# Sliding attention beside a gated MLP on one core: block 2 summed before the tensor engine, an earlier start of the value stage, a fixed port order, and outputs by accumulating DMA

## The chip, the cores and the metric

The kernel runs on one core of a Trainium2 chip. The metric is device time in microseconds (us); most executions agree within 0.3%. The trace names the engines PE (TensorE, matrix products; PEld is its weight load), DVE (VectorE), ACT (ScalarE), POOL (GpSimd) and SP (SyncE, which issues DMAs). "L930" is line 930 of that kernel's program; the same work has another line number in another version, so the text names the work with the line.

## The reference

One layer norm feeds two branches, and both are added to x. The tensors are 2048 positions by 640 features, in bf16.

```python
def reference(A_x, A_wqkv, A_wo, B_x, B_w_gate, B_w_up, B_w_down):
    x = A_x
    xn = _layernorm(x)
    return x + attention(xn, A_wqkv, A_wo) + mlp(xn, B_w_gate, B_w_up, B_w_down)

# attention (shortened): 32 heads of 20 features; position s looks at
# s, s-2, s-4, ... s-14 (8 places), softmax over these 8, then @ wo
# mlp: (xn @ w_gate) * (xn @ w_up) @ w_down, with 1536 hidden features
```

## The kernel before

The program is built by a small list scheduler in Python: it keeps an expected clock for each engine and emits tasks in an order fixed at build time. On the chip each engine runs its own list in that order and waits on semaphores. The 2048 positions are four blocks j of 512; the 640 features are five chunks c of 128.

Logits: VectorE multiplies queries by shifted keys (8 places as two rows r of 4), and TensorE sums the 20 features of a head with a 0/1 matrix `G` of 32 columns. Four such matmuls lie side by side in the array, one for each 128 positions. In the "narrow" way each chunk gives a product tile that goes to TensorE, ten tiles for a block. In the "wide" way, used for block 3 only, VectorE makes fp32 products straight from the queries in PSUM (the memory into which TensorE writes), GpSimd and accumulating DMAs add chunks 0 to 3, and TensorE gets four tiles: two sums and two of chunk 4.

```python
QUAD = {3: (1, 0)}                       # blocks whose rows 1 and 0 go the wide way
ORDER = ((0, "n"), (1, "n"), (2, "n"), (3, "n"), (3, "w"))
...
# logits(j, slots): four tiled matmuls for each product tile
for a in range(4):
    o = PS[32 * a:32 * a + 32, b, :].rearrange("p (q s) -> p q s", q=4)
    ... e.matmul(o, G[:], x, ..., tile_position=(0, 32 * a))
```

Values: after a softmax (one for blocks 0 and 1, one for 2 and 3) VectorE multiplies attention by values for each of 20 units (one unit is a block and a chunk), GpSimd adds the two rows of places, and TensorE sums the remaining four with a 0/1 matrix `SEL`, in batches of units.

```python
BATCH = (1, 4, 9, 14, 19)                # last unit of each batch of value sums
def calm():                              # GpSimd keeps off while a softmax has begun
    return all(("sm", x) in done or count.get(("logits", x), 0) < 2 for x in range(2))
```

Output: for each tile of 128 positions, `dn` runs 12 matmuls with `w_down` and 5 with `wo` into one PSUM bank; VectorE adds x (`fin`, out of a small ring `XR`) into `FOUT`, and a DMA stores it.

## Time and profile before

| | before |
|---|---|
| device time, median of 4 | 268.65 us (268.47 to 268.70) |
| span of the profiled execution | 266.8 us |
| first projection matmul starts | 6.21 us |
| last add of an output starts | 264.27 us |
| busy: PE, VectorE, ScalarE, GpSimd | 98%, 82%, 40%, 50% |
| tiled runs on PE (4 of logits, 5 of value sums) | 9 |

A "tiled run" here is an unbroken stretch of matmuls with `G` or `SEL`, between full-width matmuls. The busy share says which engine has the least room, but not whether PE's matmuls are fast; for that one divides a stretch's time by its matmuls. The chain that ended last tells which work sets the end. The lines are in the prediction below.

### The profile page before, as it was taken

The numbers are of one execution on the slowest core, as the hardware profiler recorded it, in microseconds if no ns is written. First come the engines' busy times: TensorE is split into PE (matmuls) and PEld (weight loads), VectorE is DVE, ScalarE is ACT, GpSimd is POOL, SyncE is SP. The second block draws the span as 40 slices with busy tenths as digits, with TensorE's granted clock in tenths as the row PEclk, the third lists the DMA queues.
The fourth block names the chain that finished last, engine by engine and source line by source line (L and its number), as shares of the span: only waits on it lengthen the run. The fifth ranks groups of instructions, "written<-read, shape, count | busy, mean of one in ns | idle before, by whom it ended". The sixth has DMA issues, their size and how long they took to land.

```text
span 266.8 us, 4468 instructions
## 1 busy us (share of the span) xinstructions
PE 261.3 (98%) x1771; PEld 152.6 (57%) x1788; DVE 218.3 (82%) x278; ACT 107.6 (40%) x193; POOL 132.4 (50%) x83
## 2 busy tenths in 40 slices
PE   7999999999999999999999999999999999999996
PEld 5996965444444444444444446764577547754775
DVE  4678899999999996379999899988998999981221
ACT  3469998556732122255434442007500460016000
POOL 1000000000007359700399999977999799979000
PEclk9999999999999999999999999999999999999999
DMA  7974789502226997193426733656345633130101
GB/s 213 374 207 81 195 107 371 213 0 98 101 49 161 192 234 178 9 333 81 114 49 142 170 80 87 185 162 168 80 129 152 184 96 89 49 98 2 49 27 49
DMA packets 40933, 35.75 MB, mean 134 GB/s; under 512 B 16080, under 2 KB 39120, under 8 KB 40912
## 3 DMA queue, kind: packets, MB, share of 16 engines
q1 hardware_dynamic: 40096, 33.31, 46.0%
q0 software_dynamic: 576, 2.10, 4.1%
q8 instruction: 14, 0.23, 0.4%
q10 hardware_dynamic: 240, 0.05, 0.1%
q14 instruction: 7, 0.06, 0.1%
HBM read 25.07 MB, written 5.26 MB: 114 GB/s over the span
## 4 chain that ended last, share of the span: by engine, by line
PE 96%; DVE 1%; DMA 1%; issue 1%; ACT 0%
PE PS L1195 39%; PE PS L1277 28%; PE PS L655 22%; PE PS L930 3%; PE PS L687 2%; PE PS L1144 2%; DMA XST<-in_A_x_dram 1%; PE PS L599 0%; DVE STATS L542 0%; ACT XNT L611 0%; DVE XNS L563 0%; DVE XNT L609 0%; DVE FOUT L1290 0%; ACT SD L548 0%; DVE MV L545 0%
## 5 line engine op out<-in xcount | busy, mean ns | idle before, releaser
L1096 POOL TENSOR_TENSOR SV<-PV 128x1024 bf16<-128x1024 f32 x40 | 93.2, 2361 | 20.4 <-DVE LOG L981 19.4
L1091 DVE TENSOR_TENSOR PV<-VX,PS 128x1024 f32<-128x1024 bf16 (+1 forms) x56 | 91.9, 1669 | 2.5 <-POOL SV L1096 2.3
L655 PE MATMUL PS<-XNT,WQKV 128*128 128x512 bf16 (+2 forms) x384 | 60.2, 315 | 0.4 <-issue 0.2
L1195 PE MATMUL PS<-XNT,WG 128*128 128x512 bf16 x238 | 59.4, 379 | 0.2
L1195 PE MATMUL PS<-XNT,WU 128*128 128x512 bf16 x231 | 57.7, 379 | 0.4 <-issue 0.2
L655 PEld LDWEIGHTS PS<-XNT,WQKV 128*128 128x128 bf16 x390 | 37.9, 112 | 21.8 <-ACT LOG L941 0.8
L1195 PEld LDWEIGHTS PS<-XNT,WG 128*128 128x128 bf16 x240 | 23.3, 98 | 28.5 <-issue 0.8
L1195 PEld LDWEIGHTS PS<-XNT,WU 128*128 128x128 bf16 x240 | 23.4, 98 | 28.2 <-ACT LOG L941 0.4
L819 DVE TENSOR_TENSOR PRD<-QT,KT 128x2048 bf16<-128x2048 bf16 x32 | 36.8, 1215 | 0.0
L1290 DVE TENSOR_TENSOR FOUT<-PS,XR 128x320 bf16<-128x320 f32 (+1 forms) x33 | 15.7, 477 | 18.4 <-PE PS L1277 18.3
L1277 PE MATMUL PS<-WD,HT 128*128 128x320 bf16 x192 | 28.5, 299 | 0.0
L660 ACT ACTIVATE HT<-PS 128x512 bf16<-128x512 f32 x24 | 14.3, 596 | 31.6 <-PE PS L1195 31.6
L1277 PE MATMUL PS<-WO,OT 128*128 128x320 bf16 (+1 forms) x165 | 26.6, 295 | 0.0
L890 POOL TENSOR_TENSOR PRF<-PRF,PRF 128x1024 f32<-128x1024 f32 x4 | 9.4, 2348 | 31.2 <-DVE PRF L864 31.2
L660 ACT ACTIVATE UX<-PS 128x512 bf16<-128x512 f32 x14 | 8.4, 597 | 39.5 <-PE PS L1195 39.5
L949 POOL MEMSET LOG<- 32x6 bf16 (+6 forms) x7 | 0.4, 96 | 47.6 <-ACT LOG L941 47.6
L1204 DVE TENSOR_TENSOR HT<-HT,PS 128x512 bf16<-128x512 bf16 x23 | 15.7, 684 | 9.5 <-PE PS L1195 7.4
L1277 PEld LDWEIGHTS PS<-WD,HT 128*128 128x128 bf16 x192 | 18.6, 98 | 8.0 <-issue 0.4
L1277 PEld LDWEIGHTS PS<-WO,OT 128*128 128x128 bf16 x165 | 15.9, 98 | 5.9
L864 DVE TENSOR_TENSOR PRF<-PS,KT 128x1024 f32<-128x1024 f32 x16 | 19.0, 1216 | 0.3 <-DMA PRF<-PRF 0.3
L660 ACT ACTIVATE XNT<-PS 128x512 bf16<-128x512 f32 x12 | 7.2, 598 | 25.5 <-PE PS L1195 25.5
L542 DVE BATCH_NORM_STATS2 STATS<-XST 128x6 f32<-128x320 bf16 x32 | 14.6, 472 | 2.5 <-DMA XST<-in_A_x_dram 2.5
(62 smaller groups left out, 235.7 us busy)
## 6 DMA issues: line engine op xcount, KB each, us to landing
VX<-v_scratch SPq DMA_DIRECT2D x80, 130.0 KB, 2.9
XST<-in_A_x_dram SPq DMA_DIRECT2D x16, 160.0 KB, 5.7
v_scratch<-VST SPq DMA_DIRECT2D x4, 640.0 KB, 4.2
XR<-in_A_x_dram SPq DMA_DIRECT2D x16, 160.0 KB, 2.7
out_dram<-FOUT SPq DMA_DIRECT2D x15, 160.0 KB, 1.8
PRF<-PRF POOLq DMA_DIRECT2D x4, 512.0 KB, 8.7
WG<-in_B_w_gate_dram SPq DMA_DIRECT2D x1, 1920.0 KB, 8.6
WU<-in_B_w_up_dram SPq DMA_DIRECT2D x1, 1920.0 KB, 12.0
```

The costliest lines, as they stand in the source:

```text
L542: op("dve", lambda e: e.bn_stats(o, a), r=[a], w=[("st", t, i)], name=f"bn{t}_{i}", occ=0.49)
L655: op("pe", (lambda o, l, x, c, first: lambda e: e.matmul(o, l, x, start=first, stop=(c == NCH - 1)))(o, l, x, c, first), r=[l, x], w=[o], ...
L660: X = op("act", (lambda o, i: lambda e: e.activation(o, i, ACT.Copy))(o, i), r=[i], w=[o], name=name, occ=0.12 + n * 0.9e-3)
L819: op("dve", lambda e: e.tensor_tensor(s[:], qb, kv, ALU.mult), r=[q, rk], w=[s[:]], name=f"prod{j}_{r}_{c}", occ=1.15, lock=True)
L864: X = op("dve", lambda e: e.tensor_tensor(o[:], qb, kv, ALU.mult), r=[q, rk], w=[o[:]], name=f"prow{j}_{r}_{c}_{q0}", occ=1.17)
L890: yield Task("pool", lambda: op("pool", lambda e: e.tensor_tensor(x, x, y, ALU.add), r=[x, y] + tokens(), w=[x], name=name, occ=2.36, lock ...
L1091: op("dve", lambda e: e.tensor_tensor(p, vw, a, ALU.mult), r=[vv] + rk, w=[p], name=f"pv{u}_{x}_{r0}", occ=0.09 + 1.1 * nr)
L1096: X = op("pool", lambda e: e.tensor_tensor(o, p[:, :, 0, :], p[:, :, 1, :], ALU.add), r=[p[:]] + tokens(), w=[o], name=f"pva{u}_{x}", occ= ...
L1195: op("pe", (lambda l, x, c: lambda e: e.matmul(PS[:, b, :], l, x, start=(c == 0), stop=(c == NCH - 1)))(l, x, c), r=[l, x], w=[PS[:, b, :] ...
L1204: X = op("dve", lambda e: e.tensor_tensor(h, h, PS[:, hold[1], :], ALU.mult), r=[h, PS[:, hold[1], :]], w=[h], name=f"h{m}_{j}", occ=0.65)
L1277: op("pe", (lambda l, x, i: lambda e: e.matmul(dst, l, x, start=(i == 0), stop=(i == n - 1)))(l, x, i), r=[l, x], w=[PS[:, b, :]], name=f" ...
L1290: X = op("dve", lambda e: e.tensor_tensor(o, PS[:, b, 0:wid], xr, ALU.add), r=[PS[:, b, :], xr], w=[o], name=f"fin{t}_{nb}", occ=0.15 + wi ...
```

## The change

The intent is fewer matmuls for block 2's logits. The diff is long; this is its core, and cuts are marked. "Port" in it means the memory port that VectorE and GpSimd share (point (3) of what the prediction cites).

```diff
-    QUAD = {3: (1, 0)}
+    QUAD = {2: (1, 0), 3: (1, 0)}
-    ORDER = ((0, "n"), (1, "n"), (2, "n"), (3, "n"), (3, "w"))
+    ORDER = ((0, "n"), (1, "n"), (2, "n"), (3, "n"), (2, "w"), (3, "w"))
...  # fixed port order: a "lock" operation waits for the other engine's last one
+        if lock:
+            deps.update({d.idx: d for d in self.port["pool" if eng == "dve" else "dve"]})
...  # values ahead of softmax 2: GpSimd may work if it ends before VectorE needs the port
-    def calm():
-        return all(("sm", x) in done or count.get(("logits", x), 0) < 2 for x in range(2))
+    def room(occ, ready=0.0):
+        def f():
+            if count.get(("logits", 0), 0) >= 2 and ("sm", 0) not in done:
+                return False
+            return due[0] == INF or max(K.t["pool"], K.t_lock, ready) + occ <= due[0] + SLIP
+        return f
+    calm = room(2.36)
-    BATCH = (1, 4, 9, 14, 19)
+    BATCH = (1, 4, 6, 9, 11, 14, 19)
...  # outputs of blocks 0 to 2: x copied to the output once, results added by DMA
+        def copy_x():
+            ... op("sp", lambda e: e.dma_start(o, i), w=[("outx",)], dma=True, name="outx", nbytes=2e6)
+        def fin_act():
+            K.free_bank(hold[0], evac([(o, PS[:, hold[0], 0:wid], wid)], f"fin{t}_{nb}"))
+        def add_out():
+            ... e.dma_start(d, f, accum_op=ALU.add), r=[f, ("outx",)]
+            if j < 3:
+                yield Task("act", fin_act, r=[PS[:, hold[0], :]], w=[o], prio=6)
+                return
...  # square roots of the layer norm in pairs of tiles, SEL built on GpSimd, new buffers
```

More of the change, by code (lines that the diff above doesn't have):

```diff
@@ L64, in __init__ @@
         self.t_lock = 0.0
+        self.port = {"dve": [], "pool": []}
         self.t_data = 0.0
@@ L122, in deps_of @@
             for q in rds:
-                if inorder and q.eng == eng and not q.dma and eng != "dve":
+                if inorder and q.eng == eng and not q.dma and eng != "dve" and not (eng == "act" and k[0] == "ps"):
                     continue
@@ L195, in op @@
                 X.event = (g[0], 16)
+        if lock:
+            self.port[eng] = [X] if eng == "dve" else self.port[eng] + [X]
+            if eng == "dve":
+                self.port["pool"] = []
         self.ops.append(X)
@@ L391, in build_kernel @@
     SV += [sb("SV3", [128, 4, JB], at=a_qk + 33024), sb("SV4", [128, 4, JB], at=a_qk + 33024 + 4096)]
-    SV += [sb(f"SV{5 + i}", [128, 4, JB], at=a_ra + i * 4096) for i in range(3)]
-    sv_free = list(range(NS))
+    SV += [sb("SV5", [128, 4, JB], at=a_ra + 6 * D * 2)]
+    sv_free = [3, 4, 0, 1, 2]
     a_sc = place[0]
@@ L414, in build_kernel @@
     PRD32 = [K.sbuf(f"PRF{i}", [128, 2, JB], FP32, K.base[p.name]) for i, p in enumerate(PRD)]
-    QUAD = {3: (1, 0)}
+    QUAD = {2: (1, 0), 3: (1, 0)}
     BY_DMA = (((0, 0), (0, 2)), ((1, 0), (1, 2)))
-    NXR = 3
     a_xr = place[0]
-    XR = sb("XR", [128, NXR, D])
-    FOUT = sb("FOUT", [128, 2, D])
+    FB0 = sb("FB0", [128, 5, D])
+    FB1 = sb("FB1", [128, 2, D], at=a_ra)
+    XR = sb("XR", [128, 4, D], at=a_ra + 2 * D * 2)
     NXN = 5
@@ L440, in ht @@
             return XNT[:, m % NCH, m // NCH * JB:(m // NCH + 1) * JB]
-        return HX[HXM[m]][:] if j == 2 else HT[:, j, m, :]
+        if j == 2:
+            return OT[:, 3, m - 8, :] if m >= 8 else HX[HXM[m]][:]
+        return HT[:, j, m, :]
     HXM = (0, 1, 2, 3, 8, 9, 10, 11, 4, 5, 6, 7)
@@ L474, in build_kernel @@
        r=[IDENT[:]], w=[IDENT[:]], name="ident", occ=0.4)
+    op("pool", lambda e: e.memset(SEL[:], 0.0), w=[SEL[:]], name="sel", occ=0.1)
+    for q in range(4):
+        op("pool", (lambda q: lambda e: e.affine_select(SEL[:], SEL[:], pattern=[[-1, 32]], compare_op=ALU.not_equal, fill=1.0,
+                                                        base=-32 * q, channel_multiplier=1))(q),
+           r=[SEL[:]], w=[SEL[:]], name=f"sel{q}", occ=0.2)
     op("pool", lambda e: e.memset(G[:], 0.0), w=[G[:]], name="g0", occ=0.2)
@@ L518, in loads @@
         yield t(w, WU, B_w_up)
+        def copy_x():
+            a, b = ohbm[0:3 * JB, :], xhbm[0:3 * JB, :]
+            o, i = a.rearrange("(p r) n -> p (r n)", p=128), b.rearrange("(p r) n -> p (r n)", p=128)
+            op("sp", lambda e: e.dma_start(o, i), w=[("outx",)], dma=True, name="outx", nbytes=2e6)
+        yield num(2, "lg")
+        yield t(copy_x)
     def late_loads():
@@ L545, in aggr @@
             op("dve", lambda e: e.bn_aggr(mv, st), r=[("st", t, 0), ("st", t, 1)], w=[("mv", t)], name=f"bnag{t}", occ=0.2)
+        ts = next((g for g in GROUPS if t in g), (t,))
+        t0, t1 = ts[0], ts[-1] + 1
         def sqrt():
-            op("act", lambda e: e.activation(sd, mv[:, 1:2], ACT.Sqrt, bias=EPSC[:, 0:1]), r=[("mv", t), EPSC[:]],
-               w=[("sd", t)], name=f"sd{t}", occ=0.25)
-            mark("sd", t)
+            o, i = SD[:, t0:t1, 0:1], MV[:, t0:t1, 1:2]
+            op("act", lambda e: e.activation(o, i, ACT.Sqrt, bias=EPSC[:, 0:1]), r=[("mv", k) for k in ts] + [EPSC[:]],
+               w=[("sd", k) for k in ts], name=f"sd{t}", occ=0.25)
+            for k in ts:
+                mark("sd", k)
         def recip():
-            op("dve", lambda e: e.reciprocal(rstd, sd), r=[("sd", t)], w=[("rstd", t)], name=f"rstd{t}", occ=0.16)
-            mark("rstd", t)
+            o, i = SD[:, t0:t1, 1:2], SD[:, t0:t1, 0:1]
+            op("dve", lambda e: e.reciprocal(o, i), r=[("sd", k) for k in ts], w=[("rstd", k) for k in ts], name=f"rstd{t}", occ=0.16)
             if t >= N_DVE_A:
-                op("dve", lambda e: e.tensor_scalar(nmr, mv[:, 0:1], rstd, -1.0, op0=ALU.mult, op1=ALU.mult),
-                   r=[("mv", t), ("rstd", t)], w=[("nmr", t)], name=f"nmr{t}", occ=0.13)
+                n, m = SD[:, t0:t1, 2:3], MV[:, t0:t1, 0:1]
+                op("dve", lambda e: e.scalar_tensor_tensor(n, m, -1.0, o, op0=ALU.mult, op1=ALU.mult),
+                   r=[x for k in ts for x in (("mv", k), ("rstd", k))], w=[("nmr", k) for k in ts], name=f"nmr{t}", occ=0.13)
+            for k in ts:
+                mark("rstd", k)
         def apply():
@@ L584, in front @@
         yield Task("dve", aggr, r=[("st", t, 1)], prio=p)
-        yield Task("act", sqrt, r=[("mv", t)], prio=p - 1)
-        yield Task("dve", recip, r=[("sd", t)], prio=p)
+        mark("mv", t)
+        if t == ts[-1]:
+            yield Task("act", sqrt, r=[("mv", t)], prio=p - 1)
+            yield Task("dve", recip, r=[("sd", t)], prio=p)
+        yield have("rstd", t)
         if t >= NXN:
@@ L777, in slot @@
         return n
-    def calm():
-        return all(("sm", x) in done or count.get(("logits", x), 0) < 2 for x in range(2))
+    INF = 1e9
+    due = [INF]
+    def room(occ, ready=0.0):
[5 more added lines that the diff above has]
+    calm = room(2.36)
     def tokens():
-        return [("tok", x) for x in range(2) if ("sm", x) in done]
+        return []
     def k_view(j, r, c, q0, nq):
@@ L793, in products @@
         holds = {}
-        for j, kind in ORDER:
+        for at, (j, kind) in enumerate(ORDER):
             if kind == "w":
@@ L799, in products @@
             else:
-                if len(QUAD.get(j, ())) == 2 and j not in holds:
+                if len(QUAD.get(j, ())) == 2 and j not in holds and (j, "w") == ORDER[at + 1]:
                     yield from fetch(j, 0, holds.setdefault(j, {c: [] for c in range(4)}))
@@ L806, in products @@
                 K.spawn(logits(j, rows[j]))
+        mark("products")
     def narrow(j, r, c, slots):
@@ L833, in copy @@
         def copy():
-            evac([(QT[:, j, c, :], PS[:, hold[0], :], JB)], f"qev{j}_{c}")
+            o, i = QT[:, j, c, :], PS[:, hold[0], :]
+            op("act", lambda e: e.activation(o, i, ACT.Copy), r=[i], w=[o, ("qev", j, c)], name=f"qev{j}_{c}", occ=0.58)
             for _ in range(4):
@@ L855, in wide @@
                     yield lambda: len(hold[c]) > 0 and len(usable(j)) > 0
+                    yield num(4, "qk", 0, j, c)
                     k = slot(j)
@@ L863, in go @@
                     def go(o=o, qb=qb, kv=kv, q=q, rk=rk):
-                        X = op("dve", lambda e: e.tensor_tensor(o[:], qb, kv, ALU.mult), r=[q, rk], w=[o[:]],
+                        X = op("dve", lambda e: e.tensor_tensor(o[:], qb, kv, ALU.mult), r=[q, rk, ("qev", j, c)], w=[o[:]],
                                name=f"prow{j}_{r}_{c}_{q0}", occ=1.17)
@@ L929, in go @@
                     x = s[:, :, a * TS:(a + 1) * TS]
-                    op("pe", (lambda o, x, i, a: lambda e: e.matmul(o, G[:], x, start=(i == 0), stop=(i == nt - 1),
-                                                                   tile_position=(0, 32 * a)))(o, x, i, a),
+                    op("pe", (lambda o, x, i, a, nt: lambda e: e.matmul(o, G[:], x, start=(i == 0), stop=(i == nt - 1),
+                                                                   tile_position=(0, 32 * a)))(o, x, i, a, nt),
                        r=[G[:], x], w=[o], name=f"lg{j}_{r}_{i}_{a}", occ=0.054, lat=0.4, mode=1)
@@ L958, in tt, with go @@
         def tt(o, a, b, f, name, occ):
-            return Task("dve", lambda: op("dve", lambda e: e.tensor_tensor(o, a, b, f), r=[a, b], w=[o], name=name, occ=occ,
-                                          lock=True), r=[a, b], w=[o], prio=10, lock=True)
+            def go():
+                X = op("dve", lambda e: e.tensor_tensor(o, a, b, f), r=[a, b], w=[o], name=name, occ=occ, lock=True)
+                due[0] = INF if name == "ssum3" else X.end
+            return Task("dve", go, r=[a, b], w=[o], prio=10, lock=True)
         L = LOG[x]
@@ L971, in sub @@
                occ=1.2, lock=True)
+            due[0] = INF
         def exp():
-            op("act", lambda e: e.activation(L[:], L[:], ACT.Exp), r=[L[:]], w=[L[:]], name="exp", occ=1.9)
+            X = op("act", lambda e: e.activation(L[:], L[:], ACT.Exp), r=[L[:]], w=[L[:]], name="exp", occ=1.9)
+            due[0] = X.end
         def recip():
             op("act", lambda e: e.activation(s3, s3, ACT.Ln), r=[s3], w=[s3], name="rln", occ=0.4)
-            op("act", lambda e: e.activation(R, s3, ACT.Exp, scale=-1.0), r=[s3], w=[R], name="rs", occ=0.4)
+            X = op("act", lambda e: e.activation(R, s3, ACT.Exp, scale=-1.0), r=[s3], w=[R], name="rs", occ=0.4)
+            due[0] = X.end
         def attn():
-            op("dve", lambda e: e.tensor_tensor(L[:], L[:], bc(RS[:], 8), ALU.mult), r=[L[:], R], w=[L[:], ("tok", x)], name="attn",
+            op("dve", lambda e: e.tensor_tensor(L[:], L[:], bc(RS[:], 8), ALU.mult), r=[L[:], R], w=[L[:]], name="attn",
                occ=1.2, lock=True)
+            due[0] = INF
         def move():
@@ L992, in softmax @@
         yield num(2, "logits", x)
+        if x:
+            due[0] = max([0.0] + [d.end for d in K.deps_of("dve", K.keys(L[:]), ()).values()])
         if x:
@@ L1010, in build_kernel @@
     NU = NJ * NCH
-    BATCH = (1, 4, 9, 14, 19)
+    BATCH = (1, 4, 6, 9, 11, 14, 19)
     def vx_loads():
-        yield num(NJ, "lg")
+        yield have("products")
         for u in range(NU):
@@ L1040, in weighted @@
         yield have("atx", 0)
+        yield have("products")
         def take(a, b):
@@ L1045, in weighted, with at_copy @@
         yield Task("act", take, banks=2, prio=0, contig=True)
+        for r in range(2):
+            yield Task("act", lambda: at_copy(0, r), r=[ATX[0][:, 0, r, :]], w=[PS[:, at_bank[r], :]], prio=1)
         for u in range(NU):
             yield from unit(u)
+    def at_copy(j, r):
+        o, i = PS[:, at_bank[r], :], ATX[j // 2][:, j % 2, r, :]
+        op("act", lambda e: e.activation(o, i, ACT.Copy), r=[i], w=[o], name=f"atp{j}_{r}", occ=0.55)
     def unit(u):
@@ L1056, in unit @@
             sv_free.extend(range(NS, len(SV)))
-        yield lambda: len(sv_free) > 0
+        yield lambda: len(sv_free) > 0 and (sv_free[0] in (3, 4) or count.get(("lg",), 0) >= NJ)
         sv_of[u] = sv_free.pop(0)
@@ L1072, in unit @@
         v = VX[:, u % NVX]
-        def at_copy(r):
-            o, i = PS[:, at_bank[r], :], ATX[j // 2][:, j % 2, r, :]
-            op("act", lambda e: e.activation(o, i, ACT.Copy), r=[i], w=[o], name=f"atp{j}_{r}", occ=0.55)
         def mul(x, r0, nr):
@@ L1108, in adder @@
             yield Task("pool", lambda: add(x), r=[slots[x][:]], w=[sv[:, 2 * x:2 * x + 2, :]], prio=10, lock=True)
-        if c in (0, NCH - 1):
+        if c == NCH - 1 or (c == 0 and j):
             for r in range(2):
                 if c == 0:
-                    yield Task("act", lambda: at_copy(r), r=[ATX[j // 2][:, j % 2, r, :]],
+                    yield Task("act", lambda: at_copy(j, r), r=[ATX[j // 2][:, j % 2, r, :]],
                                w=[PS[:, at_bank[r], :]], prio=1)
@@ L1137, in sums @@
             yield have("add", u)
+        if us[-1] >= 3 * NCH:
+            yield num(8, "dn", 2)
         def go(*bs):
@@ L1163, in on_pool @@
     def on_pool(j, m):
-        return ("sm", 1) in done and m < 11 and ucount[0] - count.get(("hp",), 0) < HP_MAX
+        return count.get(("lg",), 0) >= NJ and m < 11 and ucount[0] - count.get(("hp",), 0) < HP_MAX
     def gu(j):
@@ L1186, in gu @@
                 yield num(NJ, "lg")
-            if j == 2 and m == 8:
-                yield have("atx", 1)
             hold = []
@@ L1220, in pmul @@
                     def pmul():
-                        op("pool", lambda e: e.tensor_tensor(h, h, us, ALU.mult), r=[h, us], w=[h], name=f"hp{m}_{j}",
+                        op("pool", lambda e: e.tensor_tensor(h, h, us, ALU.mult), r=[h, us] + tokens(), w=[h], name=f"hp{m}_{j}",
                            occ=1.15, lock=True)
@@ L1227, in after @@
                     yield num(k0, "hp")
-                    yield calm
+                    yield room(1.15)
                     yield Task("pool", pmul, r=[h, us], w=[h], prio=HP_PRIO, lock=True)
@@ L1238, in xr_loads @@
     def xr_loads():
-        yield have("xnt", NT - 1)
-        yield have("vx", NVX)
-        for t in range(NT):
-            if t >= NXR:
-                yield have("out", t - NXR)
-            yield Task("sp", lambda: dma(XR[:, t % NXR, :], xhbm[t * TS:(t + 1) * TS, :], w=[XR[:, t % NXR, :]], name=f"xr{t}"),
-                       prio=15, w=[XR[:, t % NXR, :]])
+        yield num(8, "dn", 0)
+        for st in range(4):
+            t = 12 + st
+            yield Task("sp", lambda: dma(XR[:, st, :], xhbm[t * TS:(t + 1) * TS, :], w=[XR[:, st, :]], name=f"xr{t}"),
+                       prio=15, w=[XR[:, st, :]])
             mark("xr", t)
@@ L1256, in dn @@
             pieces = ((0, 320), (320, 480), (480, 640)) if t == NT - 1 else ((0, 320), (320, 640))
-            yield have("xr", t)
+            if j == 3:
+                yield have("xr", t)
             yield lambda: count.get(("ot", j), 0) >= NCH or ("gu", NJ - 1) in done
@@ L1266, in dn_piece @@
         n = NF + NCH
-        o, xr = FOUT[:, t % 2, cols], XR[:, t % NXR, cols]
+        F, ft = (FB1, t % 2) if j == 3 else (FB0, t % 4)
+        o, xr = F[:, ft, cols], XR[:, t % 4, cols]
         def part(lo, hi):
@@ L1292, in fin @@
             K.free_bank(b, X)
+        def fin_act():
+            K.free_bank(hold[0], evac([(o, PS[:, hold[0], 0:wid], wid)], f"fin{t}_{nb}"))
+            bump("fin", j)
+            if count["fin", j] == 8:
+                K.one(Task("pool", add_out, r=[F[:, 0:4, :]], prio=5))
+        def add_out():
+            d = ohbm[j * JB:(j + 1) * JB, :].rearrange("(t p) n -> p t n", p=128)
+            f = F[:, 0:4, :]
+            stores.append(op("pool", lambda e: e.dma_start(d, f, accum_op=ALU.add), r=[f, ("outx",)], w=[("out", j)], dma=True,
+                             name=f"oadd{j}", occ=0.88, acc=4))
         def store():
@@ L1297, in store @@
             else:
-                f, d = FOUT[:, t % 2, :], ohbm[t * TS:(t + 1) * TS, :]
+                f, d = F[:, ft, :], ohbm[t * TS:(t + 1) * TS, :]
             stores.append(dma(d, f, r=[f], name=f"odma{t}_{nb}", eng="act" if nb == 1 and t == NT - 1 else "sp"))
@@ L1311, in dn_piece @@
         K.spawn(tail())
+    SLIP = 0.3
     N_PE_T = 4
     BN_AFTER = (4,)
+    GROUPS = ((4, 5), (6, 7), (8, 9), (10, 11), (12, 13), (14, 15))
     N_DVE_A = 6
@@ L1341, in misc @@
         yield have("xnt", NT - 1)
-        def sel():
-            for q in range(4):
-                a, b = SEL[32 * q:32 * q + 32, :], IDENT[32 * q:32 * q + 32, 32 * q:32 * q + 32]
-                op("dve", (lambda a, b: lambda e: e.tensor_copy(a, b))(a, b), r=[b], w=[a], name=f"sel{q}", occ=0.1)
         def preload(e):
@@ L1351, in misc @@
         free.append(NPR - 1)
-        yield Task("dve", sel, prio=19)
         yield Task("act", lambda: op("act", preload, name="exp_preload", occ=1.3), prio=6)
```

## The prediction

> **What bounds the kernel now.** I read the busy table of the page first, then what TensorE waited for, then the chain that ended last, and only then the other engines. The first fence has the busy line of the page, the slice line of TensorE (PE), and the whole list of PE's waits.
>
> ```profile
> PE 261.3 (98%) x1771; PEld 152.6 (57%) x1788; DVE 218.3 (82%) x278; ACT 107.6 (40%) x193; POOL 132.4 (50%) x83
> PE   7999999999999999999999999999999999999996
> PE PS L639 <- DVE ZERO L469: 1.3, 1, 1.3
> PE PS L687 <- DVE XNT L609: 0.3, 1, 0.3
> PE PS L655 <- issue: 0.2, 1, 0.2
> PE PS L1195 <- issue: 0.2, 1, 0.2
> ```
>
> The reader should see that PE waits for data only at the very start; every later need of it is met before it comes. But busy time can hide slow matmuls, so I checked the rate. In the stretch from 120 to 140 us there are 92 matmuls of 512 columns (gate and up products, L1195), 20 us / 92 = 217 ns each; a set of five takes 1.08 us in the timeline, 216 ns each. In the output stage 136 matmuls of 320 columns take 18.58 us, 136.6 ns each. Column for column these are the same rate, so nothing is hidden in the middle. The span of 266.8 us is 6.2 us of start (first projection matmul at 6.21), 258.0 us of PE at its pace, and 2.6 us from the last matmul to the end of the last store. The second fence is from the chain in order of time (start, length, what).
>
> ```profile
> 59.25 2.27 PE PS L930 x40
> 61.52 0.16 issue
> ...
> 114.73 0.98 PE PS L930 x16
> ...
> 141.64 0.61 PE PS L1144 x8
> ...
> 159.63 0.76 PE PS L1144 x12
> ...
> 244.42 1.19 PE PS L1144 x20
> 245.61 18.64 PE PS L1277 x153
> 264.25 0.02 issue
> 264.27 0.33 DVE FOUT L1290
> ```
>
> L930 is the head sum of the logits (32-column stationary, four tiles side by side): 40 matmuls for a block of ten product tiles, 16 for block 3, whose products are already added over four chunks. L1144 sums the weighted values. So a change helps only by giving PE fewer columns, fewer switches, or a shorter start or end; the other engines matter only if they come late.
>
> **What the Trainium skill says.** (1) "TensorE: Matmul & The Clock Gate", section "Wait — 56ns, not 53.3ns?", gives N / 2.4 GHz plus about 2.5 ns for a warm matmul, 215.7 ns at N = 512. The trace agrees (216 ns), so PE is at its floor. (2) "TensorEngine Tiling (Array Packing)", "Key Properties": tiles run independently, and a change of tiling mode drains the engine. The trace agrees: 40 tiled matmuls in 2.27 us are 57 ns each instead of 216, and a 0.16 us gap follows such a run. (3) "SBUF — State Buffer", in its terms, calls the port pair shared by VectorE and GpSimd an exclusive lock held for a whole instruction. I take it as the reason for a fixed order; no wait of this trace shows it alone, but POOL idled 19.4 us until the last multiply of softmax 2 (L981), by the program's own order. (4) "DMA: Bandwidth & Descriptors", "Rules for kernel authors": an accumulating DMA reads its destination and writes it later, so earlier writers must have landed. The kernel waits for the copy of x into the output; its four accumulating DMAs now landed in 8.1 to 8.9 us.
>
> **The change part by part.** The third fence has the groups that it touches (busy us, mean ns, then idle before and its releaser).
>
> ```profile
> L819 DVE TENSOR_TENSOR PRD<-QT,KT 128x2048 bf16<-128x2048 bf16 x32 | 36.8, 1215 | 0.0
> L864 DVE TENSOR_TENSOR PRF<-PS,KT 128x1024 f32<-128x1024 f32 x16 | 19.0, 1216 | 0.3 <-DMA PRF<-PRF 0.3
> L890 POOL TENSOR_TENSOR PRF<-PRF,PRF 128x1024 f32<-128x1024 f32 x4 | 9.4, 2348 | 31.2 <-DVE PRF L864 31.2
> L1096 POOL TENSOR_TENSOR SV<-PV 128x1024 bf16<-128x1024 f32 x40 | 93.2, 2361 | 20.4 <-DVE LOG L981 19.4 <-DVE PV L1091 0.8
> L1290 DVE TENSOR_TENSOR FOUT<-PS,XR 128x320 bf16<-128x320 f32 (+1 forms) x33 | 15.7, 477 | 18.4 <-PE PS L1277 18.3
> ```
>
> Block 2 over four chunks: its logits go from 40 matmuls to 16, as block 3's already did. The two rows of the chain price this directly: 2.27 - 0.98 = 1.29 us off PE. This is the only PE work that goes. The queries' projections of block 2 stay; they merely remain in PSUM. The other engines pay: VectorE makes 8 bf16 products fewer and 16 fp32 ones more, net 8 x 1.216 = 9.7 us; GpSimd gets 4 sums and 4 closing sums, 8 x 2.348 = 18.8 us, and 4 DMA issues of 0.9 us, 3.6 us.
>
> Values ahead of softmax 2: the built order has 4 value products before softmax 2 on VectorE and the value adds close behind the last closing sum on GpSimd, where before only 2 products and one add stood ahead of the 19.4 us idle. It fills that idle; PE columns stay. But the batches of value sums on PE go from 5 to 7, so two more runs in tiled mode. A run costs what is left at zero matmuls: L930's slope is 1.29 us / 24 = 0.054 us, so 0.98 - 16 x 0.054 = 0.12 us, plus up to 0.16 us of gap. I take 0.2 us each, +0.4 us on PE.
>
> Outputs by accumulating DMA: 24 of 33 final adds leave VectorE, 24 x 0.487 = 11.7 us, and become copies on ScalarE. A 512-column copy there takes 0.597 us and a 256-column one about 0.4, so I estimate 0.45, in all 10.8 us on an engine that is 40% busy. x is copied to the output by one DMA of 2 MB, 12 small loads of x vanish, and GpSimd issues 3 large adds at 0.9 us, 2.7 us. The last block keeps its add and store, so the 2.6 us at the end stay.
>
> Smaller parts: the square roots go in pairs from tile 4 (6 reciprocals fewer at 0.163 us, 5 scalings fewer at 0.214, 2.1 us off VectorE by 35 us), the selector is built on GpSimd at the start (0.7 us off VectorE), and 10 gated products instead of 14 are on GpSimd (4 x 0.685 = 2.7 us to VectorE, 4 x 1.16 = 4.6 us off GpSimd). The order of PE up to the first long run of 256-column matmuls is the same, so the start stays at 6.2 us.
>
> Sums: VectorE 9.7 - 11.7 - 2.1 - 0.7 + 2.7 = -2.1, to about 216 us; GpSimd 18.8 + 3.6 + 2.7 - 4.6 = +20.5 plus about 1 for the selector, to about 154 us. Both stay below PE, so they count only where they make PE late. PE: -1.29 + 0.4 = -0.9 us. Without any new wait: 268.65 - 0.9 = 267.75 us.
>
> **The rivals.** (a) GpSimd becomes what PE waits for. In the fence from GpSimd's timeline (start, length) its last value adds end at 239.76 + 4.66 = 244.42 us, the very time at which PE starts to sum them (chain above): the slack is nil already.
>
> ```profile
> 239.76 4.66 POOL L1096 TENSOR_TENSOR SV<-PV 128x1024 bf16<-128x1024 f32 x2
> ```
>
> After the change the closing sums of block 3 end late. VectorE, free from about 33 us, has 24 x 1.14 of bf16 products, 6.1 of softmax 1, 32 x 1.155 of fp32 products and 18 x 0.61 of gated ones ahead of them, 114.5 us; GpSimd's last sums then run to about 128 us. From there 40 x 2.335 + 8 x 1.13 + 3 x 0.9 = 105 us of its work, and 6 us in which softmax 2 has the port, give 239 us, against PE's arrival near 243.4. So some 4 us of slack for waits on copies (it idled 6.1 us for those before): it may fit and may just miss. Also its third DMA issue stands before its last add and waits for all copies of block 2. This would add 0 to 3 us. (b) The logits come earlier on PE: in the built order block 0's stand 10 and block 1's 15 matmuls of 512 columns sooner, at about 45.0 and 55.9 us, and VectorE's 10th and 20th product end at about 33 + 11.4 = 44.4 and 33 + 22.8 = 55.8 us. Each may cost PE some tenths, 0 to 1 us in all; for it speaks the thin margin, against it that the old order had about as little at block 0. (c) All falls into slack and better: PE also loses its small gaps after runs; 0.3 to 0.7 us more, 267.0 us. (d) Lighter VectorE and filled GpSimd bring a large gain, as their shares suggest. Against it stand PE's rate and its list of waits: nothing is there to regain but the start and the end. It would need 263 us.
>
> **Range and chances.** The sum is 267.75; (c) pulls down by half a microsecond, (a) and (b) up by an expected half. I predict 267.7 us. Low end 266.4: full logit gain, no extra switch cost, shorter gaps. High end 270.0: GpSimd late by 2 to 3 us. Two per cent is 5.4 us, which PE's columns can't give (3%); slower by that much needs a chain of VectorE and GpSimd that slips by over 6 us (3%). The rest, 94%, is within 2%.
>
> **What would show it.** Right: the logit group has 112 matmuls and some 6.7 us on the chain instead of 8; blocks 2 and 3 cost about 1 us each there; PE's waits stay under 1.5 us beyond the start; the 19.4 us idle of GpSimd before L981 is gone; GpSimd's busy time is near 154 and VectorE's near 216 us; the last store still ends 2.6 us after the last matmul. Wrong: PE rows with a wait for VectorE's products at the logits, for GpSimd's value sums at the selector matmuls, or for a PSUM bank that ScalarE frees late; an end that waits for an accumulating DMA; or a start shorter than 6.2 us, for which I see no cause.

## The result and the profile after

The changed kernel took 267.94 us in the median of 4 runs (267.84 to 268.03), against 268.65. The ratio is the mean time of one kernel's runs over that of the other's of the same rounds, so not quite the ratio of the quoted medians: 0.9975, with a 95% interval of 0.9957 to 0.9992. Run again in a later session, on chip 9 (`changed_again` below), it was 267.77 against 268.48, ratio 0.9970 (0.9956 to 0.9983). The gain is small and real, 0.7 us: both intervals leave out 1.

The busy line of the page and PE's complete waits, in the changed kernel:

```profile
PE 260.7 (98%) x1747; PEld 151.8 (57%) x1764; DVE 217.0 (82%) x249; ACT 112.0 (42%) x203; POOL 154.5 (58%) x99
PE PS L672 <- DVE ZERO L478: 1.3, 1, 1.3
PE PS L688 <- issue: 0.5, 3, 0.2
PE PS L720 <- DVE XNT L642: 0.3, 1, 0.3
PE PS L1253 <- ACT HX L693: 0.2, 1, 0.2
```

PE has 24 matmuls fewer and nothing new to wait for except 0.2 us for a PSUM bank. GpSimd gained 22 us of work and VectorE lost 1, and neither shows in the time.

The chain that ended last, in order of time (start, length, what). L976 is now the logits, L1204 the value sums:

```profile
56.25 2.27 PE PS L976 x40
...
100.72 0.98 PE PS L976 x16
...
129.88 0.98 PE PS L976 x16
...
166.15 0.76 PE PS L1204 x12
...
177.33 0.55 PE PS L1204 x8
...
243.82 1.19 PE PS L1204 x20
245.01 18.64 PE PS L1335 x153
263.65 0.02 issue
263.67 0.33 DVE FB L1348
```

Block 2's logits at 100.72 us now take 0.98 us, as block 3's do. Short value sums of 8 matmuls stand between output pieces, which is what the batches 5 to 6 and 10 to 11 became. The end is as before: the last output piece of 18.64 us, then one add on VectorE and its store. (The tool that draws this chain goes through ScalarE between 21 and 36 us here; PE's own list of waits above shows that PE lost nothing there.)

The groups that answer to those of before (busy us, mean ns, then idle ahead of them and its releasers):

```profile
L910 DVE TENSOR_TENSOR PRF<-PS,KT 128x1024 f32<-128x1024 f32 x32 | 37.8, 1216 | 0.3 <-PE PS L688 0.3
L936 POOL TENSOR_TENSOR PRF<-PRF,PRF 128x1024 f32<-128x1024 f32 x8 | 18.8, 2359 | 21.8 <-DVE LOG L1033 20.6 <-DVE PRF L910 1.1
L1154 POOL TENSOR_TENSOR SV<-PV 128x1024 bf16<-128x1024 f32 x40 | 95.0, 2535 | 9.6 <-DVE LOG L1033 3.3 <-DVE SM L1006 3.2 <-DVE LOG L1019 3.1
L693 ACT ACTIVATE FB<-PS 128x320 bf16<-128x320 f32 x24 | 10.5, 438 | 41.1 <-PE PS L1335 38.4 <-DMA out_dram<-FB 2.6
```

The fp32 products doubled at the same price. The idle of GpSimd before its value adds fell from 20.4 to 9.6 us; what is left are three waits of some 3 us for parts of softmax 2, whose place the fixed order sets. The output copies on ScalarE took 0.438 us each.

Where the 0.8 us between the two profiled spans went can be split in three, all in us. The start of the first projection is read from PE's timeline, the start of the last add from the chain; the middle is their difference.

| kernel | start to first projection | middle | last add to end | tiled runs |
|---|---|---|---|---|
| before | 6.21 | 258.06 | 2.53 | 9 |
| changed | 6.39 | 257.28 | 2.33 | 11 |
| changed_again | 6.39 | 257.30 | 2.31 | 11 |
| no_quad2 | 6.33 | 258.47 | 2.30 | 11 |
| many_batches | 6.25 | 259.48 | 2.37 | 21 |
| six_batches | 6.39 | 257.01 | 2.30 | 10 |

The middle lost 0.78 us, against the prediction's 0.9 us. The start is longer by 0.18 and the end shorter by 0.20, so they cancel. The start moved between 6.2 and 6.4 us among kernels whose first instructions on PE are the same; I don't read a cause into it. The 0.2 us at the end is in every profile of the changed family, also in `dve_outputs` below, whose outputs go the old way (2.33 us); its cause stays open.

### The profile page after: what moved, and what is told of

It is laid out like the page before. It is cut to its first block, busy times and chain, and to the rows that moved or that the text cites. A ratio compares the mean times of both kernels' runs of the same rounds, so it can differ in the third digit from the quotient of the medians.

```text
span 266.0 us, 4403 instructions
## 1 busy us (share of the span) xinstructions
PE 260.7 (98%) x1747; PEld 151.8 (57%) x1764; DVE 217.0 (82%) x249; ACT 112.0 (42%) x203; POOL 154.5 (58%) x99
## 4 chain that ended last, share of the span: by engine, by line
PE 92%; ACT 5%; issue 1%; DVE 0%
PE PS L1253 39%; PE PS L1335 28%; PE PS L688 17%; ACT XNS L599 3%; PE PS L976 2%; PE PS L720 2%; PE PS L1204 2%; PE PS L672 2%; ACT QT L693 1%; ACT VST L693 1%; PE PS L632 1%; ACT KT L693 1%; ACT SD L574 0%; ACT HX L693 0%; DVE XNT L642 0%
## 5 line engine op out<-in xcount | busy, mean ns | idle before, releaser
L1154 POOL TENSOR_TENSOR SV<-PV 128x1024 bf16<-128x1024 f32 x40 | 95.0, 2535 | 9.6 <-DVE LOG L1033 3.3
L1253 PE MATMUL PS<-XNT,WG 128*128 128x512 bf16 x235 | 58.6, 379 | 0.3
L910 DVE TENSOR_TENSOR PRF<-PS,KT 128x1024 f32<-128x1024 f32 x32 | 37.8, 1216 | 0.3 <-PE PS L688 0.3
L936 POOL TENSOR_TENSOR PRF<-PRF,PRF 128x1024 f32<-128x1024 f32 x8 | 18.8, 2359 | 21.8 <-DVE LOG L1033 20.6
L693 ACT ACTIVATE FB<-PS 128x320 bf16<-128x320 f32 x24 | 10.5, 438 | 41.1 <-PE PS L1335 38.4
L863 DVE TENSOR_TENSOR PRD<-QT,KT 128x2048 bf16<-128x2048 bf16 x24 | 27.3, 1217 | 0.0
L1262 DVE TENSOR_TENSOR HT<-HT,PS 128x512 bf16<-128x512 bf16 x24 | 16.4, 685 | 8.0 <-PE PS L1253 7.9
L954 POOL TENSOR_TENSOR PRD<-PRF,PRF 128x1024 bf16<-128x1024 f32 x8 | 18.7, 2354 | 0.9 <-DVE PRF L910 0.8
L1348 DVE TENSOR_TENSOR FB<-PS,XR 128x320 bf16<-128x320 f32 (+1 forms) x9 | 4.1, 454 | 15.3 <-PE PS L1335 15.3
```

The lines of the kernel that those rows point to most:

```text
L693: X = op("act", (lambda o, i: lambda e: e.activation(o, i, ACT.Copy))(o, i), r=[i], w=[o], name=name, occ=0.12 + n * 0.9e-3)
L863: op("dve", lambda e: e.tensor_tensor(s[:], qb, kv, ALU.mult), r=[q, rk], w=[s[:]], name=f"prod{j}_{r}_{c}", occ=1.15, lock=True)
L910: X = op("dve", lambda e: e.tensor_tensor(o[:], qb, kv, ALU.mult), r=[q, rk, ("qev", j, c)], w=[o[:]], name=f"prow{j}_{r}_{c}_{q0}", occ=1.17)
L936: yield Task("pool", lambda: op("pool", lambda e: e.tensor_tensor(x, x, y, ALU.add), r=[x, y] + tokens(), w=[x], name=name, occ=2.36, lock ...
L954: yield Task("pool", lambda: op("pool", lambda e: e.tensor_tensor(o, a, y, ALU.add), r=[a, y] + tokens(), w=[o], name=f"qend{j}_{r}_{q0}", ...
L1154: X = op("pool", lambda e: e.tensor_tensor(o, p[:, :, 0, :], p[:, :, 1, :], ALU.add), r=[p[:]] + tokens(), w=[o], name=f"pva{u}_{x}", occ= ...
```

## The experiments

Every experiment gave a correct result. The two probes repeat an instruction with the same result. "Unplanned" means that the scheduler was told that the extra instruction takes no time, so that every engine's order stays as it was. The reserve of PSUM banks that I raised in three runs (`DN_KEEP` 3 to 5, where the plan otherwise finds no end) changes nothing in the changed kernel: its order comes out the same line for line. Every edit other than the probes and `no_port_order` lets the scheduler build a new order, so such a run undoes a part together with the order that the part led to. The smaller parts (square roots in pairs, `SEL` on GpSimd, fewer gated products on GpSimd, new buffers) were undone in no run; what they are worth is not shown.

### no_quad2: the wide way of block 2 undone

```diff
-    QUAD = {2: (1, 0), 3: (1, 0)}
+    QUAD = {3: (1, 0)}
-    ORDER = (..., (3, "n"), (2, "w"), (3, "w"))
+    ORDER = (..., (3, "n"), (3, "w"))
```

> The changed kernel with block 2 multiplied chunk by chunk again, all else as changed. Theory A (the shorter logits of block 2 are the only thing that TensorE gained): its group of tiled logit matmuls goes back to 136, block 2's run from 0.98 to 2.27 us, and the time rises by 1.29 us to 269.2 us, above the kernel before, since the two extra runs of value sums stay. Rival B (the gain came from the lighter VectorE, the filled GpSimd or the outputs): the time stays at 267.9 us within 0.3.

It took 268.93 us, ratio 1.0010 to the kernel before (0.9997 to 1.0022), and so about 1.0 us over the changed kernel, 0.3 us under theory A's figure. Its group of logits:

```profile
L976 PE MATMUL PS<-PRD,G 128*32 128x512 bf16 x136 | 8.1, 380 | 0.0
```

This is the 136 matmuls and 8.1 us of before (6.8 us in the changed kernel), and the middle in the table rises by 1.19 us. VectorE fell to 204.4 us, far lighter than before the change, and GpSimd to 138.3 us, 16 us less than in the changed kernel (132.4 before the change), and the time did not follow. So theory A holds and rival B falls: undoing the shorter logits gives back the whole gain and a little more. Against the kernel before, the middle is longer by 0.41 us, with the same logits and two more tiled runs. That fits the 0.4 us of the prediction, but does not show it alone, as the other parts differ too; `many_batches` below prices a run.

### only_quad2: the wide way of block 2 alone, in the kernel before

```diff
-    QUAD = {3: (1, 0)}
+    QUAD = {2: (1, 0), 3: (1, 0)}
...  # ORDER as in the change, and two repairs that let two blocks go the wide way
-    DN_KEEP = 3
+    DN_KEEP = 5
```

> The kernel before with block 2's products added over four chunks and nothing else of the change (one reserve of PSUM banks raised from 3 to 5, or its plan finds no end; in the changed kernel that number alters no instruction). Theory A says that this part alone gives TensorE its 1.29 us but makes GpSimd late: 18.8 us of sums and 3.6 us of issues come before the value adds, which still wait for softmax 2, so they start some 10 to 16 us later and TensorE waits for them at the last value sums: 277 to 283 us. Rival C (the parts are independent of each other): 268.65 - 1.29 = 267.4 us.

It took 286.94 us, ratio 1.0683: 18 us slower. First the largest wait of PE, then the first value adds of GpSimd after softmax 2 in the timeline (start, length, idle before in brackets):

```profile
PE PS L1144 <- POOL SV L1096: 8.0, 4, 3.8
147.63 4.67 POOL L1096 TENSOR_TENSOR SV<-PV 128x1024 bf16<-128x1024 f32 x2 [18.54 <-DVE LOG L981]
```

In the kernel before, these adds start at 131.05 us. They are now 16.6 us late, as block 2's added products and sums pushed block 3's logits back (from 114.73 to 131.31 us on the chain) and the adds still wait for all of softmax 2. GpSimd also waited 11.4 us for value products of VectorE, so both helpers were late. PE waited 8.0 us for value adds, 3.4 us for ScalarE, in all 12.9 us more than before. Its mean granted clock (the share of full speed that the profile shows) fell to 0.976, and 12 output matmuls behind the last waits took 3.41 us in place of 1.79; I don't split the 18 us further. Theory A holds in kind; my range ended 4 us too low. The part that yields all of the gain costs 18 us without the others: they buy it the room.

### values_late: the value products only after softmax 2

```diff
         yield have("atx", 0)
         yield have("products")
+        yield have("sm", 1)
```

> The changed kernel with the value products held back until softmax 2 is done. Theory A: GpSimd's head start of four to six adds is lost, softmax 2 ends near 141 us and the value adds start near 143 us instead of 127.5 (with 9.6 us of waits after it), so the last ones end about 6 us later and TensorE waits for them: 272 to 274 us, the wait in front of the last value sums. Rival B (GpSimd is not the bound, its idle costs nothing): 267.9 us within 0.5.

It took 277.39 us, ratio 1.0327, 9.5 us over the changed kernel and above my range. PE's timeline near the end:

```profile
252.31 1.25 PE L1336 MATMUL PS<-WD,XNT 128*128 128x320 bf16 x4 [7.38 <-POOL XNT L1280]
253.48 2.32 PE L1205 MATMUL PS<-SV,SEL 128*32 128x512 bf16 x20
```

PE waited 7.38 us at one place, for GpSimd's last gated products, which queue behind its value adds. What I had left out is the second line: the 20 value sums after the wait took 2.32 us here and 1.26 us in the timeline of the changed kernel, and the granted clock was 0.73 from 240 to 256 us and 0.50 from 248 to 256. The Trainium skill, "TensorE: Matmul & The Clock Gate", section "What's actually happening", says that the array falls back to half its clock after an idle window of about 3.4 us; the wait was longer than that and the matmuls after it slower by a factor of 1.8, so this trace agrees. A wait of TensorE of this length costs more than itself.

### dve_outputs: all outputs the old way

```diff
-            if j < 3:
-                yield Task("act", fin_act, r=[PS[:, hold[0], :]], w=[o], prio=6)
-                return
...  # XR and FOUT as before, x loaded tile by tile, copy_x gone, DN_KEEP = 5
```

> The changed kernel with all outputs as before: x loaded tile by tile, final adds on VectorE, no accumulating DMA, no copy of x (bank reserve 5). Theory A: VectorE gets back 24 x 0.487 = 11.7 us between 168 and 240 us, where it had only some 4.5 us of waits for GpSimd; GpSimd loses about 5 us of issues and waits. VectorE's value products get late by 3 to 7 us and TensorE waits at the last value sums: 270 to 274 us. Rival (the output part is neutral, both engines have room): 267.9 us within 0.5.

It took 274.66 us, ratio 1.0224, 6.7 us over the changed kernel. VectorE was busy 225.4 us (217.0). The chain of waits near the end goes from output adds to value products on VectorE, from there to value adds on GpSimd, and from there to PE:

```profile
PE PS L1202 <- POOL SV L1152: 3.8, 2, 1.9
```

GpSimd waited 4.6 us for value products, PE 3.8 us for value adds. Most of the rest is slow matmuls: the 17 output matmuls from 251.22 to 255.69 us took 4.47 us, where 137 ns each make 2.3. The granted clock was 0.60 and 0.54 in the two stretches of 4 us from 248 to 256, though no single wait was longer than 1.91 us: two stood close together, with two matmuls between them. So waits shorter than that of `values_late` can slow TensorE too; with the 1.1 and 0.4 us of `pool_probe` below the clock stayed at 1.00. The outputs by DMA thus take no matmul off PE and are still needed: 24 adds on VectorE make its value products late, and those GpSimd.

### no_port_order: the waits of the fixed order taken out

```diff
-        if lock:
-            deps.update({d.idx: d for d in self.port["pool" if eng == "dve" else "dve"]})
```

> The changed kernel without the semaphore waits that fix the order of VectorE and GpSimd at their shared port; the order of instructions on every engine is the same. Theory A: TensorE's columns are untouched and both engines mostly run in the planned order anyway, so 267.9 us within 0.3; at most a GpSimd add slips in front of softmax 2 on VectorE and delays it, with the median or the spread of times a few tenths worse. Rival D (the fixed order is what holds the plan together): over 269 us or a wide spread.

My expectation failed. It took 270.21 us, ratio 1.0058 (1.0045 to 1.0070), 2.3 us over the changed kernel, with a narrow spread (270.06 to 270.42). The order of instructions is the same, and no data need was touched. A sum of softmax 2 on VectorE (start, length), first in the changed kernel, then in this run, with a gated product of GpSimd beside it:

```profile
144.18 1.22 DVE L1006 TENSOR_TENSOR SM<-LOG 128x1024 f32<-128x1024 bf16 x1
```

```profile
145.76 3.03 DVE L1004 TENSOR_TENSOR SM<-LOG 128x1024 f32<-128x1024 bf16 x1
147.65 2.15 POOL L1277 TENSOR_TENSOR HX<-HX,UX 128x512 bf16<-128x512 bf16 x1
```

Here GpSimd's value add before that product ran from 145.34 to 147.70 us, and the sum ended 1.1 us after that; the gated product, 1.16 us long in the changed kernel, ended 1.0 us after the sum. Each took about its usual time once the other was done. The Trainium skill, "SBUF — State Buffer", the terms, describes such a lock of the port pair that VectorE and GpSimd share, held for a whole instruction; the prediction could only cite it, and these times agree with it. VectorE's busy time rose from 217.0 to 224.2 us: instructions of the softmax that took 0.4 to 1.2 us in the changed kernel hang for up to 3 us while GpSimd works, and two of the three gated products among them took 2.14 and 2.15 us. Here waiting in the instruction was not cheaper than waiting on a semaphore, and the slips did not stay in slack. PE waited 1.2 us for a bank that VectorE freed late, and then inside its next value sums for GpSimd: the projections behind these started at 169.23 in place of 166.91 us, 2.3 us late, and PE stayed so late to the end.

### pool_probe, pool_probe_old and dve_probe: how much slack is left

```diff
+            if u == 17 and x == 0:      # one value add twice, planned as 0 us
+                op("pool", ..., r=[p[:]], w=[o], name="probe", occ=0.0)
```

> The changed kernel with one value add on GpSimd done twice (same inputs, same output), three units before the end, about 2.35 us, not known to the plan: every engine keeps its order. If GpSimd has no slack before the last value sums, the time rises by 2 to 2.35 us to about 270.1 us, with a wait of TensorE in front of them. If it has the 4 us of slack of the prediction's rival (a), the time stays at 267.9.

> The kernel before with one value add on GpSimd done twice, three units before the end, about 2.35 us, not known to its plan. The prediction read nil slack from its last value adds ending at 244.42 us as TensorE started to sum them. If so, +1.8 to 2.35 us as in the changed kernel's probe (which rose by 1.1 us over the kernel before, 1.8 over the changed one): about 270.7 us. If GpSimd idles for copies anyway before the end (its 1.9 us wait at 238 us), the probe is partly hidden: 268.7 to 269.5 us.

> The changed kernel with one value product on VectorE done twice at the same place, about 2.2 us, order kept. VectorE waits for GpSimd 4.5 us in all among its value products, so theory A expects that it has room: 267.9 us within 0.5. If VectorE is as tight as GpSimd, the time rises by up to 2.2 us to 270.1.

The extra 2.35 us on GpSimd cost the changed kernel 1.8 us (269.78 us, ratio 1.0042), and PE shows the wait in front of value sums:

```profile
PE PS L1206 <- POOL SV L1156: 1.1, 1, 1.1
```

The same probe cost the kernel before only 0.43 us (268.91 us, ratio 1.0012). So GpSimd had about 1.9 us of slack before and has about 0.5 us now. The prediction's "nil already" was wrong for the kernel before, and this line of its GpSimd timeline tells why:

```profile
238.65 1.16 POOL L1221 TENSOR_TENSOR XNT<-XNT,UX 128x512 bf16<-128x512 bf16 x1 [1.87 <-ACT UX L660]
```

GpSimd idled 1.87 us for a copy just before its last two value adds. With the probe, that idle is gone and the last adds end at 245.17 us in place of 244.42. So an engine that ends just in time has not used up its slack if it idled shortly before for something else.

The extra 2.2 us on VectorE cost 0.8 us (268.70 us, ratio 1.0003, against 0.9970 to 0.9975 for the changed kernel). I had expected nothing. Its waits for GpSimd add up to 4.5 us in the changed kernel, but they come in pieces of up to 1.0 us; that they can therefore cover only part of a delay this late is my reading, no run tests it.

### many_batches, six_batches and changed_again: the price of a tiled run

```diff
-    BATCH = (1, 4, 6, 9, 11, 14, 19)
+    BATCH = tuple(range(20))            # many_batches
+    BATCH = (1, 4, 6, 9, 14, 19)        # six_batches, with DN_KEEP = 5
```

> The changed kernel with every unit's value sums on their own, 21 tiled runs on TensorE in place of 11, columns unaltered. Theory A (a run costs 0.2 us) expects +2.0 us: 269.9 us. If a switch of tiling mode costs nothing once the queue is full, 267.9 us; if it costs as much as the 0.16 us gap plus a drained pipe at both ends, about 0.4 us each, 272 us.

> The changed kernel with the value sums in six batches in place of seven (units 10 to 14 in one; bank reserve 5): one tiled run fewer on TensorE, 10 instead of 11. Theory A prices a run at 0.2 us and expects 267.7 us, the best of all, if GpSimd isn't made late by value buffers that come free later; if it is, TensorE waits in front of the last value sums and the time is 268 us or over.

> The changed kernel itself, unaltered, once more beside the others of this call, as their base on the same chip: 267.9 us within 0.2, 0.7 us below the kernel before.

All three ran on one chip. The changed kernel took 267.77 us, the one with 21 runs 269.79, the one with 10 runs 267.57 (ratio 0.9962 to the kernel before, 0.9950 to 0.9975). The value sums of the changed kernel and of many_batches:

```profile
L1204 PE MATMUL PS<-SV,SEL 128*32 128x512 bf16 x80 | 5.6, 383 | 0.0
```

```profile
L1204 PE MATMUL PS<-SV,SEL 128*32 128x512 bf16 x80 | 7.4, 388 | 0.0
```

The same 80 matmuls, and in both profiles (`changed_again` and this) PE waits for nothing after the first 9 us, so the 2.02 us are the ten more runs: 0.20 us each. One run fewer gave 0.20 us back. That settles a price which the prediction had pieced together from one slope and one gap. It also gives a kernel that beats both, if only by a little: six batches, 267.57 us, its runs (267.50 to 267.69) just touching those of the changed kernel (267.69 to 267.93).

### quad123: block 1 the wide way too

```diff
-    QUAD = {2: (1, 0), 3: (1, 0)}
+    QUAD = {1: (1, 0), 2: (1, 0), 3: (1, 0)}
```

> The changed kernel with block 1 too added over four chunks. TensorE saves another 1.29 us. Theory A: VectorE gets 9.7 us and GpSimd 22 us more before the value adds, where neither has slack left, so TensorE waits for the last value adds and the time is over 272 us, up to 285. Rival B (engines below TensorE's share do not count): 266.6 us.

It took 306.82 us, ratio 1.1419, worse than the range that I gave. PE waited in five groups, 23.6 us in all, the largest for GpSimd's products in the last block:

```profile
PE PS L1335 <- POOL XNT L1279: 7.4, 1, 7.4
```

The granted clock fell to 0.933. PE also waited for ScalarE and VectorE; the 39 us are not split into their parts here. In this form the next 1.29 us is not to be had; that no other order could have it is not shown.

## Why the prediction was right, point by point

**The bound.** It said that only columns, switches, the start and the end of PE count. no_quad2 shows it: with 13 us less work on VectorE and 16 us less on GpSimd than the changed kernel has, the time rose.

**The logits, -1.29 us.** Shown: the run of block 2 fell from 2.27 to 0.98 us, and undoing this part returned 1.19 us of the middle and 1.0 us of the median.

**Two more runs, +0.4 us.** Many_batches shows it, with 0.20 us for a run. The 0.41 us of the middle between no_quad2 and the kernel before agrees; in their times the difference is within the noise (ratio 0.9997 to 1.0022). The prediction read its 0.16 us gap as following "such a run", and it does so behind only two of the nine runs of the kernel before (59.25 and 76.74 us); that 0.2 us came out right is partly luck.

**The sum, 267.75 us.** Measured 267.94 and 267.77. The middle lost 0.78 us in place of 0.9. Two of its signs did not come: the start was 6.39 us in place of 6.2, and the end came 2.35 us after the last matmul in place of 2.6; the two cancel.

**The other engines.** VectorE was to reach about 216 us and reached 217.0; GpSimd 154, and 154.5; a copy of outputs 0.45 us, and 0.438. The issue of an accumulating output DMA was put at 0.9 us; it is recorded with 1.3, but GpSimd's next add starts 0.82 to 0.84 us after it begins, so the term holds.

**Rival (a), GpSimd late.** It did not happen, but by about 0.5 us only, and that it did not is partly luck, as two terms were off. The slack in the kernel before was not nil but 1.9 us. And the end of the last value add was put at 239 us; GpSimd's timeline in the changed kernel has

```profile
241.10 2.85 POOL L1154 TENSOR_TENSOR SV<-PV 128x1024 bf16<-128x1024 f32 x1
243.41 2.75 POOL L1279 TENSOR_TENSOR XNT<-XNT,UX 128x512 bf16<-128x512 bf16 x2
```

It is recorded to 243.95 us, and the next instruction starts at 243.41, just as PE came at 243.82. The Trainium skill, "Perfetto Trace Analysis", section "GPSIMD Engine Instruction", says to time GpSimd by the spacing of starts and not by the recorded span. This trace agrees: after the first output DMA the value adds are recorded with up to 2.87 us, while six of them between 222.23 and 236.13 us are 2.32 us apart, no slower than before. So the end came over 4 us later than predicted: GpSimd waited 9.6 us around softmax 2, where 6 were allowed, and 1.1 us for copies ahead of the output DMAs, which the prediction had named as uncertain. The start of the value adds was right: the last sum for block 3 ended at 127.57 us, 128 predicted.

**Rival (b), earlier logits.** They came at 45.22 and 56.25 us, predicted 45.0 and 55.9, and cost no wait on PE.

**Rival (c), smaller gaps.** They did not get smaller: 0.16 to 0.18 us follow three of the four runs of logits in the changed kernel (those at 45.22, 56.25 and 100.72 us).

**Rival (d), a large gain.** The range left it out rightly.

**What the prediction missed.** It treated the other parts as neutral for PE and asked only whether they would make it late. They are the condition of the gain. Each removed alone costs 2.3 us (port order), 6.7 us (outputs) or 9.5 us (values ahead), and the gain alone, without them, costs 18 us. Its 3% for "slower" was a statement on this build, in which everything fits by half a microsecond, not on the margin of the idea.

## What to carry to other kernels

Where one engine is at its floor, count what it must still do, its columns and its switches of mode, and price a change by those; the busy shares of the others give no gain, only the room that the change may use up. Before moving work from the bound engine to a helper, measure the helper's slack with one unplanned extra instruction shortly before the deadline: here 2.35 us told 1.9 us of slack from 0.5, which the end time of its last add did not. Judge such a change whole, since the part that yields the gain can be the part that loses most when it is tried alone.

## What the Trainium skill lacked or had wrong

- "TensorEngine Tiling (Array Packing)", "Key Properties", says that a change of tiling mode drains TensorE and gives no price. Here a run of 32-column tiled matmuls between full-width ones cost 0.20 us beyond its matmuls (2.02 us for ten more runs).
- "SBUF — State Buffer" describes the lock of the shared port, but has no figure for what leaving the order to it costs a kernel. Here each engine held up the other in turn: a VectorE sum took 3.03 us in place of 1.22, two gated products of GpSimd 2.14 and 2.15 us in place of 1.16, and the kernel lost 2.3 us against an order fixed by semaphores.
- "DMA: Bandwidth & Descriptors" has no time for an accumulating DMA. Here one of 640 KB into HBM landed in 6.8 to 10.2 us and is recorded with 1.3 us on GpSimd, whose next add starts 0.82 to 0.84 us after the issue begins; one of 512 KB within SBUF is recorded with 0.86 us in the mean.
